# Linear attention and two MLPs on one core: a third chunk buffer, one load of the decays, weights loaded into their place, and an order of engines written out for the first layer

## The chip, the core and the metric

The kernel runs on one core of a Trainium2 chip. The metric is the time of one execution on the device in microseconds (us), as the median of several executions. One more execution is taken by the hardware profiler; its page and its trace are what is read below. The engines of the core are PE (matrix multiply, with its weight loads as PEld), DVE (VectorE), ACT (ScalarE), POOL (GpSimd) and SP (SyncE, which here issues the DMAs).

## What is computed

A gated linear attention over 4 x 8 heads of 768 tokens with head size 48, then two MLPs over 3072 tokens (width 384, inner width 2048), the first with the gate h * sigmoid(1.702 h), the second with h - tanh(h). All in float32.

```python
for t in range(S):
    state = alpha[:, :, t, :, None] * state + einsum('bhd,bhe->bhde', k[:, :, t], v[:, :, t])
    y[:, :, t] = einsum('bhd,bhde->bhe', q[:, :, t], state)
x = y.transpose(0, 2, 1, 3).reshape(B * S, H * D)
h = x @ w_in;   x = (h / (1 + exp(-1.702 * h))) @ w_out      # first MLP
h = x @ w_in2;  out = (h - tanh(h)) @ w_out2                 # second MLP
```

## The kernel before

**Attention in chunks.** A chunk is 128 tokens of one batch entry with all 8 heads, so there are 24 chunks (`NG`), six to a batch entry (`NCH`). Within a chunk the recurrence is written as matrix products: `a_scan` makes running products of the decays, one forward and one backward over the chunk (tensor_tensor_scan on DVE), `a_scale` multiplies k and q by them, PE makes the scores k by q (`a_scores` for chunks 0 to 7, two halves of eight matmuls each, `a_whole` for the later ones), a mask is laid on (a select on POOL, or a multiply on DVE at L301 in `a_whole`), and `a_out` makes the outputs: L325 with the carried state, L332 from scores and v, L341 the addition to the state, which `a_state` folds in on DVE. `a_guard` sums squares of the decay products on ACT for a check of range. For chunks from 8 on (`FULL`), `a_scale` runs on POOL and `a_turn` transposes k on DVE, 16 small transposes a chunk.

**Through memory and back.** `a_evac` copies a chunk's outputs from PSUM (ACT, L360) and stores them with four DMAs (L365) to a DRAM tensor; `a_back` reads them back token-transposed (L378); `a_x` splits x into a high part (ACT, L382) and a low part (DVE, L383) in the reduced float32 format that PE multiplies fast.

**The MLPs in blocks and steps.** Tokens go in six blocks of 512 for each layer, and a block has 16 steps, one for each 128 of the inner width; 192 steps in all. Step s makes nine matmuls of `gemm1` (L392: three parts of the contraction, each as high*high, high*low, low*high), then the activation (`sig_1`, L406, ACT) and its split (`g_split`: ghi on ACT at L409, glo on DVE at L410), and the nine matmuls of `gemm2` (L399) for step s - 3 (`LAG`).

**Weights.** They come as float64 bits. `w_load` fetches 768 KB into one of three `raw` buffers, `w_bits` and `w_join` make float32 on DVE (L163, L164, L176), `w_split` gives whi (ACT, L193) and wlo (DVE, L194). `conv` advances this pipeline by one weight at each call. `w_check` tests the exponents of a weight (DVE, then ACT) after loading it a second time.

**What runs when.** Chunks 0 to 3 are done ahead of block 0. During the steps of block j of the first layer the four chunks of block j + 1 are worked on (`attend`, `a_done`), so block 0 has chunks 4 to 7 and all the weight conversions between its steps, and blocks 1 to 4 have four chunks each. The checks of the first layer's weights lie in blocks 2 and 3, eight in each. The second layer's weights are converted in block 5 and in the second layer's first block.

**Buffers.** Two chunk buffers (`late`) and, for chunk 2 alone, a third place in tiles that are free at the start. `a_done(g)` loads chunk g + 2. The decays of a chunk are loaded twice, in reversed and in forward order (2 x 516 of 2056 columns).

**Order.** `in_order(begin)` fixes the order of each engine as the code emits it up to the end of block 0; behind that a scheduler orders the instructions by its own planning.

Of the kernel before, what the change touches and what calls it, by code (L numbers as in the profile page):

```python
# [17 lines left out]
C = 128  # L18
# [14 lines left out]
QW = 2 * AW + NP * C + NP * CE  # L33
# [35 lines left out]
def linear_attention_mlps(ctx, tc, xq, xv, fa, fv, cst, w1, w2, out):  # L69
# [10 lines left out]
    whi = [T(f"whi{m}", (128, WC), F32R) for m in range(MT)]  # L80
    wlo = [T(f"wlo{m}", (128, WC), F32R) for m in range(MT)]
    raw = [T(f"raw{i}", (128, WC, 2), I32) for i in range(3)]
# [18 lines left out]
    AR = 7184  # L101
# [15 lines left out]
    COLS = (AW, AW, NP * CE, NP * C, VW)  # L117
    lateb, late = [], []
    for _ in range(2):
        lateb.append(carve(QW))  # L120
        cuts = [0]
        for c in COLS[:4]:
            cuts.append(cuts[-1] + c)
        late.append([lateb[-1][:, u:v] for u, v in zip(cuts, cuts[1:])] + [carve(VW)])
    late0 = lateb[0]
    xsf = xs.rearrange("p k t -> p (k t)")
    third = [gt[:, 0:AW], gt[:, AW : 2 * AW], xsf[:, 0 : NP * CE], xsf[:, NP * CE :][:, :NB], gt[:, 2 * AW : 2 * AW + VW]]
# [27 lines left out]
    def w_load(layer, m):  # L155
        return SP.dma_start(out=raw[m % 3], in_=wsrc[layer][m].bitcast(I32).rearrange("p (n t) -> p n t", t=2))
# [4 lines left out]
    def w_bits(l, m):  # L161
        r, f = raw[m % 3], cfs[l][m % len(cfs[l])]
# [5 lines left out]
    def w_check(l, m):  # L168
        t = wt[m % 2]
        tc.keep_in_program_order(V.tensor_scalar(out=t, in0=w_high(raw[m % 3]), scalar1=0x3800, scalar2=0x7800,  # L170
# [3 lines left out]
    def w_join(l, m):  # L174
        r, f = raw[m % 3], cfs[l][m % len(cfs[l])]
        V.scalar_tensor_tensor(out=f.bitcast(I32), in0=r[:, :, 0], scalar=29, in1=f.bitcast(I32), op0=ALU.logical_shift_right, op1=ALU.bitwise_or)  # L176
# [13 lines left out]

    def w_split(l, m):
        f = cfs[l][m % len(cfs[l])]
        A.copy(whi[m], f)  # L193
        V.tensor_tensor(out=wlo[m], in0=f, in1=whi[m].bitcast(F32), op=ALU.subtract)  # L194
# [3 lines left out]

    def src(g, n):
        return (third if g == 2 else late[(g + (g > 2)) % 2])[n][: DP if n < 4 else 128]  # L200

    def dec(g, n):
        return src(g, n)
# [4 lines left out]
    def dec3(g, n):  # L208
        return pairs(dec(g, n))
# [16 lines left out]
    def a_load(g, parts=range(5)):  # L226
        if g == 0 and 0 in parts:
            for n in range(2):
                SP.dma_start(out=src(0, n), in_=xq[0, :, n * AW : (n + 1) * AW])
        elif 0 in parts:  # L230
            t = gt if g == 2 else lateb[(g + (g > 2)) % 2]
# [542 lines left out]
```

## Time and profile before

| | us |
|---|---|
| median of 3 runs | 953.19 (952.18 to 955.78) |
| profiled execution, its own time | 957.78 |
| its span | 956.1 |
| PE busy | 913.8 |
| DVE busy | 676.5 |
| ACT busy | 449.5 |
| POOL busy | 85.9 |

A line of the timeline tells when an instruction started (us from the start of the span), how long it took, its engine and line, what it writes and reads, how many of a kind are merged into the line, and in square brackets how long the engine had been idle before and who released it. Matmuls overlap in their pipeline, so the distance from one start to the next is what a matmul costs, and the time given is its latency. SPq lines are DMA issues. The windows give busy times of each engine in a stretch, with the number of instructions, and the granted clock of TensorE as a share of full speed (PEclk), which is also recorded as full where the trace has no clock record, as in the first 52 us.

### The profile page before, as it was taken

Reading aid. Unit: us, or ns where it says so; the run is one execution under the profiler, and the core shown is the slowest. Engines: PE = TensorE matmul, PEld = TensorE weight load, DVE = VectorE, ACT = ScalarE, POOL = GpSimd, SP = SyncE. Lnnn points to the kernel's source line nnn. Section 1 sums busy time; section 2 is a strip of 40 time slices with the busy share of each in tenths; the row PEclk is TensorE's granted clock in tenths of the full one; section 3 lists DMA queues with packets and bytes.
Section 4 is the critical chain, followed back from the end, with each engine's and each line's share of the span. In section 5 each row is a group of like instructions: output and inputs, shape, how many; then the busy total and the mean of one; then the engine's idle time right before and its main releaser. Section 6 shows DMA issues by size and latency. Waiting matters only on the chain.

```text
span 956.1 us, 13257 instructions
## 1 busy us (share of the span) xinstructions
PE 913.8 (96%) x4870; PEld 728.1 (76%) x4870; DVE 676.5 (71%) x1124; ACT 449.5 (47%) x906; POOL 85.9 (9%) x70
## 2 busy tenths in 40 slices
PE   5569999999989999999999999999999999999997
PEld 4347777777768777777888888888888888888885
DVE  7799997844774787484159986766776777766663
ACT  4445533323434434343344564554566566544542
POOL 1201211101120111110100200100100001000000
PEclk9999999989989999999999999999999999999999
DMA  9767434422643565434125410200322420000001
GB/s 268 236 201 240 137 87 125 120 68 79 200 132 141 159 196 198 128 113 158 32 93 181 138 60 1 78 22 1 113 96 89 166 99 1 33 1 1 34 1 37
DMA packets 58107, 101.91 MB, mean 107 GB/s; under 512 B 5024, under 2 KB 37408, under 8 KB 58032
## 3 DMA queue, kind: packets, MB, share of 16 engines
q1 hardware_dynamic: 58032, 100.97, 33.7%
q8 instruction: 40, 0.66, 0.3%
q14 instruction: 35, 0.29, 0.1%
HBM read 86.79 MB, written 14.16 MB: 106 GB/s over the span
## 4 chain that ended last, share of the span: by engine, by line
PE 61%; DVE 0%; issue 0%; ACT 0%; ACTq 0%
PE bank L399 30%; PE bank L392 29%; PE bank L332 1%; PE bank L298 0%; PE bank L325 0%; PE bank L341 0%; DVE xs L442 0%; DVE arena L301 0%; PE bank L268 0%; ACT xs L445 0%; ACTq L671 0%
## 5 line engine op out<-in xcount | busy, mean ns | idle before, releaser
L410 DVE TENSOR_TENSOR glo<-gt,ghi 128x512 fp32r<-128x512 f32 x192 | 140.1, 732 | 151.0 <-ACT ghi L409 146.8
L392 PE MATMUL bank<-xhi,whi 128*128 128x512 f32 x576 | 229.2, 398 | 9.5 <-ACT xhi L382 8.8
L399 PE MATMUL bank<-ghi,whi 128*128 128x512 f32 x576 | 233.1, 405 | 0.0
L399 PE MATMUL bank<-ghi,wlo 128*128 128x512 f32 x576 | 229.0, 397 | 0.0
L392 PE MATMUL bank<-xlo,whi 128*128 128x512 f32 x576 | 228.5, 397 | 0.4 <-DVE xlo L383 0.4
L399 PE MATMUL bank<-glo,whi 128*128 128x512 f32 x576 | 228.5, 397 | 0.0
L392 PE MATMUL bank<-xhi,wlo 128*128 128x512 f32 x576 | 228.1, 396 | 0.0
L409 ACT CAST ghi<-gt 128x512 fp32r<-128x512 f32 x192 | 119.2, 621 | 220.8 <-DVE gt L421 133.1
L392 PEld LDWEIGHTS bank<-xhi,whi 128*128 128x128 f32 x576 | 109.2, 190 | 35.6 <-ACT xhi L382 9.0
L399 PEld LDWEIGHTS bank<-ghi,whi 128*128 128x128 f32 x576 | 109.2, 190 | 28.4 <-issue 1.9
L392 PEld LDWEIGHTS bank<-xlo,whi 128*128 128x128 f32 x576 | 109.3, 190 | 26.4 <-DVE xlo L383 1.2
L399 PEld LDWEIGHTS bank<-glo,whi 128*128 128x128 f32 x576 | 109.4, 190 | 25.7
L392 PEld LDWEIGHTS bank<-xhi,wlo 128*128 128x128 f32 x576 | 109.1, 189 | 25.5
L399 PEld LDWEIGHTS bank<-ghi,wlo 128*128 128x128 f32 x576 | 109.5, 190 | 24.2 <-issue 0.5
L406 ACT ACTIVATE gt<-bank 128x512 f32<-128x512 f32 x96 | 57.4, 597 | 95.6 <-PE bank L392 72.0
L308 DVE STREAM_TRANSPOSE cf<-arena 32x128 f32<-32x128 f32 x256 | 77.5, 303 | 24.9 <-PE bank L341 10.0
L419 DVE SCALAR_TENSOR_TENSOR arena<-arena,bank 128x512 f32<-128x512 f32 x96 | 65.8, 686 | 29.4 <-ACT arena L417 28.6
L421 DVE SCALAR_TENSOR_TENSOR gt<-arena 128x512 f32<-128x512 f32 x96 | 68.3, 712 | 10.9 <-DVE arena L420 1.4
L417 ACT ACTIVATE arena<-bank 128x512 f32<-128x512 f32 x96 | 57.3, 597 | 36.1 <-PE bank L392 35.7
L243 DVE TENSOR_TENSOR_SCAN arena<-arena,seg 112x516 f32<-112x516 f32 x46 | 63.5, 1380 | 14.6 <-DMA arena<-xq 13.6
L418 ACT ACTIVATE arena<-arena,cs 128x512 f32<-128x512 f32 x96 | 69.6, 725 | 2.9
L420 DVE SCALAR_TENSOR_TENSOR arena<-arena 128x512 f32<-128x512 f32 x96 | 67.9, 707 | 3.0
(89 smaller groups left out, 663.2 us busy)
## 6 DMA issues: line engine op xcount, KB each, us to landing
raw<-w SPq DMA_DIRECT2D x64, 768.0 KB, 4.5
arena<-xq SPq DMA_DIRECT2D x46, 224.0 KB, 4.4
arena<-xq SPq DMA_DIRECT2D x22, 451.5 KB, 5.1
xlo<-xt SPq DMA_DIRECT2D x24, 192.0 KB, 4.4
x1t<-xs SPq DMA_DIRECT2D x6, 768.0 KB, 3.4
arena<-x1t SPq DMA_DIRECT2D x6, 768.0 KB, 4.5
out<-xs SPq DMA_DIRECT2D x18, 256.0 KB, 2.3
arena<-xv SPq DMA_DIRECT2D x23, 192.0 KB, 3.3
```

Of the source, the lines that this page charges most:

```text
L243: V.tensor_tensor_scan(out=dec(g, n), data0=src(g, n), data1=seg, initial=0.0, op0=ALU.mult, op1=ALU.max)
L308: V.transpose(out=d[32 * y : 32 * y + 32], in_=k[32 * x : 32 * x + 32, :, 32 * y : 32 * y + 32])
L392: P.matmul(out=h, lhsT=w[m][:, ws], rhs=x[:, k, :n], start=c == 0, stop=c == 3 * KT - 1)
L399: P.matmul(out=acc[k][:, :n], lhsT=w[m][:, ws], rhs=x[s % 3][:, :n], start=m == 0 and c == 0, stop=m == MT - 1 and c == 2)
L406: A.activation(out=gf[i][:, :n], in_=h, func=AF.Silu, scale=1.702)
L409: A.copy(ghi[s % 3][:, :n], gf[s % 2][:, :n])
L410: e.tensor_tensor(out=glo[s % 3][:, :n], in0=gf[s % 2][:, :n], in1=ghi[s % 3][:, :n].bitcast(F32), op=ALU.subtract)
L417: A.activation(out=u, in_=h, func=AF.Square, accum_out=usum[:, s - NS1 :][:, :1])
L418: A.activation(out=w, in_=u, func=AF.Square, bias=pbias)
L419: V.scalar_tensor_tensor(out=p, in0=u, scalar=P3, in1=h, op0=ALU.mult, op1=ALU.mult)
L420: V.scalar_tensor_tensor(out=p, in0=u, scalar=-PR, in1=p, op0=ALU.add, op1=ALU.mult)
L421: V.scalar_tensor_tensor(out=gf[i], in0=w, scalar=PD, in1=p, op0=ALU.add, op1=ALU.mult)
```

## The change

- The decays of a chunk are loaded once, in forward order, into 517 columns whose last is set to zero by a memset; the backward scan reads them with a negative step. `a_load` has four DMAs, for decays, q, k and v.
- Chunks from 3 on take three buffers in turn (`place_of`): the two of `late` and `spare`, which lies in the memory of two `raw` buffers. `a_done(g)` loads chunk g + 3.
- In the first layer a weight is loaded by `w_given` into the memory where its whi and wlo will lie, all 16 without a ring. The second load for the check goes to the third `raw` buffer.
- The checks of the first layer lie in blocks 1 to 4, four a block, each two steps behind its load.
- The start is written anew: all loads of chunks 0 to 3 first, the constants on ACT's DMA queue, the activation table loaded at the start, the scores of chunk g + 1 ahead of the outputs of chunk g, and `idle(n)`: n matmuls of 512 columns into an unused bank, 18 at the start, then 14, and 4, 3, 5 and 38 behind the outputs of chunks 0 to 3. Two of chunk 3's stores go to ACT's DMA queue. Three weights are converted by the start of block 0, with the bits of a fourth (before: three, a fourth joined and the bits of a fifth).
- In block 0, chunks 4 to 7 begin at steps 2, 5, 8 and 11 (before 0, 3, 6, 9), and `conv` stands at the end of a step.
- In blocks 1 to 4, `steady` places a chunk's parts at steps d = 0, 1, 2 and 5 from its begin (steps 0, 3, 7, 10 of the block). `in_order` now reaches to the end of block 4.

```diff
+    def place_of(g):
+        return third if g == 2 else (spare, *late)[g % 3] if g > 2 else late[g]
...
     def a_scan(g, n):
         if n == 0:
             V.memset(first, 1.0)
-        V.tensor_tensor_scan(out=dec(g, n), data0=src(g, n), data1=seg, ...)
-        if n == 0:
+            V.tensor_tensor_scan(out=dec(g, 0), data0=src(g, 1)[:, AW:0:-1], data1=seg, ...)
             V.reciprocal(out=first, in_=dec3(g, 0)[:, :, C:])
+        else:
+            V.tensor_tensor_scan(out=dec(g, 1), data0=dec(g, 1), data1=seg, ...)
...
     def a_done(g, b=5):
         a_evac(g, b)
-        if g + 2 < NG:
-            a_load(g + 2)
-        if g < FULL:
-            a_back(g)
+        a_back(g)
+        if g + 3 < NG:
+            a_load(g + 3)
...
+    STARTS = (0, 3, 7, 10)
+    def steady(g, d):
+        if d == 0:
+            if g == FULL:
+                a_turn(g, 0)
+            prep(g + 1, 0)
+            a_whole(g, 5)
+        if d == 1:
+            a_turn(g, 1)
+            prep(g + 1, 1)
+            prep(g + 1, 2)
+            prep(g, 3)
+        if d == 2:
+            if g + 1 < NG:
+                a_turn(g + 1, 0)
+            a_out(g, 5)
+            a_state(g)
+            a_done(g)
+        if d == 5:
+            x_hi(g)
+            x_lo(g)
...
+    def idle(n):
+        w = seg[:, 1:65].bitcast(BF16)
+        for _ in range(n):
+            P.matmul(out=bank[2], lhsT=w, rhs=w.unsqueeze(1).to_broadcast([DP, 4, 128]), start=True, stop=True)
...
     for r in range(3):
         prep(0, r)
+    idle(18)
+    for r in range(2):
+        s_mm(0, r, (5, 3)[r])
+    for x in range(4):
+        s_copy(0, x % 2, (5, 3)[x % 2], x > 1)
+    idle(14)
     for g in range(4):
         if g < 3:
             for r in range(3):
                 prep(g + 1, r)
+            for r in range(2):
+                s_mm(g + 1, r, (5, 3)[r])
...
         a_out(g, 0)
+        idle((4, 3, 5, 38)[g])
+        if g < 3:
+            for x in range(4):
+                s_copy(g + 1, x % 2, (5, 3)[x % 2], x > 1)
+        else:
+            w_hi(1, 0)
+        a_evac(g, 0, A if g == 3 else SP)
...
+            if l == 1 and 0 < j < len(L1) - 1 and m - 2 in STARTS:
+                w_check(1, 4 * (j - 1) + STARTS.index(m - 2))
+            if l == 1 and 0 < j < len(L1) - 1 and m in STARTS:
+                w_load(1, 4 * (j - 1) + STARTS.index(m), 2)
...
-        if s == MT - 1:
+        if s == (len(L1) - 1) * MT - 1:
             in_order(begin)
```

## Rows read from the trace of the kernel before

**Rows 1.** The page, part 1: busy time, share of the span, instructions of each engine.

```profile
PE 913.8 (96%) x4870; PEld 728.1 (76%) x4870; DVE 676.5 (71%) x1124; ACT 449.5 (47%) x906; POOL 85.9 (9%) x70
```

**Rows 2.** Timeline of the start: start us, us, engine, line, operation, [idle before <-releaser].

```profile
22.18 2.72 PE L279 MATMUL bank<-xs 48*128 48x176 f32 x16
30.31 2.72 PE L279 MATMUL bank<-arena 48*128 48x176 f32 x16
37.86 0.65 ACT L360 COPY wtb<-bank 112x256 f32<-112x256 f32 x2
38.26 2.61 SPq L365 DMA_DIRECT2D xt<-wtb  x4
47.41 0.80 PE L392 MATMUL bank<-xhi,whi 128*128 128x512 f32 x1 [8.79 <-ACT xhi L382]
```

**Rows 3.** Windows, blocks 0 to 5: length, busy by engine, PEclk, DMA share, GB/s.

```profile
47.41:136.35 88.94, 81.30 (x486) 62.22 (x486) 84.01 (x131) 45.27 (x99) 13.32 (x12) 0.96 0.60 178
136.35:222.98 86.63, 84.60 (x530) 66.56 (x528) 58.37 (x126) 29.59 (x55) 9.75 (x8) 0.96 0.31 89
222.98:310.21 87.23, 84.19 (x529) 66.59 (x528) 56.23 (x124) 35.29 (x70) 10.68 (x8) 0.96 0.49 151
310.21:392.64 82.43, 81.50 (x514) 64.04 (x513) 58.45 (x125) 35.06 (x70) 10.06 (x8) 1.00 0.56 174
392.64:473.42 80.78, 80.78 (x530) 64.18 (x528) 40.81 (x81) 29.78 (x56) 7.79 (x7) 1.00 0.33 106
473.42:540.34 66.92, 66.92 (x289) 54.26 (x288) 50.23 (x62) 30.91 (x49) 3.50 (x4) 1.00 0.39 130
```

**Rows 4.** Timeline of blocks 1 and 2, DVE and PE: two waits of PE.

```profile
185.56 1.23 DVE L243 TENSOR_TENSOR_SCAN arena<-arena,seg 112x516 f32<-112x516 f32 x1 [0.88 <-DMA arena<-xq]
188.45 2.27 DVE L243 TENSOR_TENSOR_SCAN arena<-arena,seg 112x516 f32<-112x516 f32 x1
191.35 0.42 PE L325 MATMUL bank<-arena,state 48*48 48x128 f32 x4 [1.45 <-DVE arena L301]
277.98 1.69 PE L325 MATMUL bank<-arena,state 48*48 48x128 f32 x16 [3.04 <-DVE arena L301]
```

**Rows 5.** Timeline of PE in block 0: dense and attention matmuls.

```profile
50.31 0.63 PE L392 MATMUL bank<-xhi,whi 128*128 128x512 f32 x1
50.73 0.63 PE L392 MATMUL bank<-xlo,whi 128*128 128x512 f32 x1
110.29 0.87 PE L279 MATMUL bank<-arena 48*128 48x176 f32 x8
115.46 0.66 PE L325 MATMUL bank<-arena,state 48*48 48x128 f32 x16
116.04 1.08 PE L332 MATMUL bank<-arena 128*48 128x128 f32 x16
116.95 0.53 PE L341 MATMUL bank<-arena 128*48 128x48 f32 x16
117.41 0.50 PE L399 MATMUL bank<-ghi,whi 128*128 128x512 f32 x1
```

**Rows 6.** Timeline of DVE in the start: chunk 0's first scan, chunk 1's memset.

```profile
4.19 1.23 DVE L243 TENSOR_TENSOR_SCAN arena<-arena,seg 112x516 f32<-112x516 f32 x1 [0.79 <-DMA arena<-xq]
8.05 0.06 DVE L242 MEMSET seg<- 112x4 f32 x1
```

**Rows 7.** Timeline of DVE in block 0: a weight's split, bits, and glo.

```profile
59.71 1.11 DVE L194 TENSOR_TENSOR wlo<-xs,whi 128x768 fp32r<-128x768 f32 x1
61.62 0.55 DVE L163 TENSOR_SCALAR cf<-raw 128x768 int32<-128x768 int32 x1
63.07 0.68 DVE L410 TENSOR_TENSOR glo<-gt,ghi 128x512 fp32r<-128x512 f32 x1
```

**Rows 8.** Timeline of POOL in the start: the select alone, and beside scans.

```profile
10.66 0.64 POOL L285 TENSOR_SCALAR_AFFINE_SELECT arena<-arena 128x512 f32<-128x512 f32 x1 [10.15 <-ACT arena L283]
24.58 2.81 POOL L285 TENSOR_SCALAR_AFFINE_SELECT arena<-arena 128x512 f32<-128x512 f32 x2 [5.33 <-ACT arena L283]
```

## What the change will do to the time

> **What bounds the kernel now.** I read the page first, then the timeline of the start for PE's longest wait, then PE's time block by block. By the page PE is the long engine, busy 913.8 of 956.1 us, and DVE comes next with 676.5 [rows 1]. So only two things can shorten the run: PE starting its main stream earlier, and PE not waiting inside it. The longest wait of PE is 8.79 us for the x of the first block, at 47.41 [rows 2]. The windows cut the span where the first L392 matmul of a block starts [rows 3]: the main stream starts at 47.41 and block 0 (16 steps of 18 matmuls, with the scores and outputs of chunks 4 to 7 between) takes 88.94 us. Blocks 1 to 4, with four chunks each, take 86.63, 87.23, 82.43 and 80.78. Block 5, without attention, takes 66.92, or 4.18 a step and 0.232 a matmul. In block 4 PE is busy 80.78 of 80.78 and the granted clock is 1.00, so that is what a block with four chunks costs when nothing waits. From 473.42 on nothing of the change touches PE, and I leave it as it is: 482.6 us to the end.
>
> Where blocks 1 and 2 lose time, the timeline shows one pattern [rows 4]. A scan at 185.56 waits 0.88 us for its load, the next scans (one of them 2.27 us long) and the mask multiplies queue behind it on DVE, and PE waits 1.45 us for the masks at 191.35. At 277.98 the same wait is 3.04 us. After each, the granted clock falls: 0.96 in those blocks against 1.00 in block 4. One such event costs the whole excess of its block, 86.63 - 80.78 = 5.85 and 87.23 - 80.78 = 6.45 us, so three quarters or half of the price is the clock and the rest the wait.
>
> **The change, part by part.** *Three buffers, loads three chunks ahead.* A chunk's load is now issued a whole chunk (about 20 us in blocks 1 to 4) before its scan, where it landed too late by 0.88 us. The DMA share in blocks 1 to 4 is 0.31 to 0.56 [rows 3], so there is room. The loads wait on SP for the buffer of a chunk that is already finished, so what stands behind them (the next chunk's stores, x read-back) is not held.
>
> *The fixed order in blocks 1 to 4.* I followed one chunk through the new order: masks are written in its first step and read in its third, the transposes in the second, the state update behind its own output matmuls, x two steps after its read-back is due. Every operand of PE is made at least one step (4.18 us) before its matmul. DVE is busy 40.81 to 58.45 us of a block [rows 3], so it has the time. The tightest place is the last chunk of a block: its x split ends about where the next block's first matmul starts; I allow nothing for it and put 1 us a block into the range. Gain: 5.85 + 6.45 + 1.65 (block 3) = 13.95 us.
>
> *Weight checks, four a block instead of eight in two blocks.* Each brings one reload on SP, one DVE and one ACT instruction; the reload stands two steps ahead of its check, on a buffer of its own. In block 4 DVE is idle for half the block. Cost nothing; if the reload were late, the DVE instruction would hold glo of its step, which PE needs two steps later.
>
> *The start.* Before, the attention of chunks 0 to 3 runs at PE's low clock: two dense matmuls at 50.31 and 50.73 are 0.42 us apart, against 0.232 later, which is the 1.2 GHz level against the 2.4 GHz one [rows 5]. The score matmuls of a chunk take 2.72 us and a chunk 8.13 (22.18 to 30.31) [rows 2]. At the high level the same matmuls cost 0.80 for half the scores, then 0.58, 0.91 and 0.46 by start to start [rows 5], so a chunk is 3.55 us of PE. The new kernel puts idle matmuls ahead and between and runs the scores of the next chunk before the outputs of this one. Then DVE sets the pace: one chunk's scans and scales take from 4.19 to 8.05, 3.86 us [rows 6], and with the state update and some contention I take 4.6, between 3.86 and 8.13. The four extra memsets (0.06 each, [rows 6]) hide in the 0.79 us that the first scan waits for its load. The reversed scan has no row. Its bounds are a scan alone, 1.23, and the longest scan, 2.27 [rows 4, 6]; I take 1.23, since the elements are as many. First outputs: 8.05 + 4.6 (chunk 1 scaled) + 1.6 (its scores) + 1.4 = 15.7; those of chunk 3 end 3 x 4.6 later, at 29.5. Before, from chunk 3's copies (37.86) to the first L392 matmul (47.41) is 9.55 us, of which 2.61 are four store issues on SP; two of them now go to ACT's queue, -1.3 [rows 2]. So x is there at 29.5 + 8.25 = 37.8. The 38 idle matmuls after chunk 3 have no row either; by the dense rows they take 38 x 0.232 = 8.8 us, or 16.0 at 0.42. I take 8.8: 29.5 + 8.8 = 38.3. **Block 0 starts at 38.2**, 9.2 us earlier.
>
> *Block 0.* Its step 3 needs weight 3 split. After x of chunk 3 (split by 38.2) DVE has in order: scans and scales of chunk 4 (3.86), the state update (two instructions on 192 columns, between nothing and two glo of 512 columns, 1.36: I take 0.7), then bits of weights 3 and 4 (1.45 each), one glo (0.68), and join and split of weight 3 (1.91) [rows 6, 7]: 10.0 us, so 48.2. PE's steps 0 to 2 take 3 x 2.09 + 0.80 = 7.1 and end at 45.3, so PE waits 2.9 us there. That is what comes next in place of the old 8.8. By [rows 4] a wait of 1.45 us was enough for a fall; I charge half of one, 1.7. The other 13 steps cost 13 x 4.18 + 4 x 1.95 (outputs) + 7 x 0.80 (scores) + 1.7 (what block 4 has over its rows) = 69.4. Block 0 ends at 48.2 + 69.4 + 1.7 = **119.3** instead of 136.35. DVE just keeps up: a weight costs 3.36, a glo 0.68, a third of a chunk 1.6, so 5.6 us a step against PE's 5.3, with the first and last steps lighter. Bounds: 114.4, if PE never waits, and 124, if DVE sets every step with another 0.3 us of contention.
>
> **The sum.** 136.35 - 119.3 = 17.05, and 13.95 in blocks 1 to 3: 31.0 us. The profiled execution took 957.78 us (1.7 around its span): 926.8. The median of the runs shown is 953.19, 4.6 lower than that execution. One clock event is 5.85 to 6.45 us, so I take the 4.6 to be such an event that comes in some executions; the changed kernel has none of them and keeps 926.8. If it is something else, the time is 4.6 lower, which the low end holds.
>
> **A rule weighed against a row.** In the start the mask select on POOL lies beside DVE's scans. Alone it takes 0.64 us; two beside a scan take 2.81 [rows 8]. *The Trainium skill, "SBUF — State Buffer", section "Who interferes with whom", says that a DVE instruction with two SBUF inputs and a GpSimd instruction that reads SBUF exclude each other for their whole length.* The rows agree with that in size: 2.81 is 1.4 each, which is 0.64 and most of a scan. In the new start every select meets a scan or a scale, since DVE is never free there. It is the third rival below.
>
> **Rivals.** *The clock stays low in the start* (chance 0.20, 936 us). For it: PE was at 1.2 GHz for the first 50 us though the window's matmuls followed each other closely, and between chunks only 3 to 5 idle matmuls stand. Then a chunk keeps its 8.13: outputs of chunk 3 end at 15.7 + 24.4 = 40.1, and the 38 idle matmuls take 8.8 to 16.0, so block 0 starts at 48.9 to 56.1, say 52. PE finds all weights ready and takes 7.1 + 69.4: 128.5, 9.2 later than my sum: 936. Against it: 18 dense matmuls stand ahead, and in the kernel before it was the first dense stream, from 47.41 on, that brought the high level.
>
> *The change does not do what it says in blocks 1 to 4* (0.10, 934 us): the scans no longer wait for loads, but the fixed order brings another wait in one or two chunks. Half of 13.95 stays: 933.8.
>
> *Scans and selects exclude each other* (0.08, 931 us): per chunk two selects of 1.4 and DVE longer by 2 x 0.64: 1.1 us on each of four chunks, and the start is 4.4 us later: 931.2.
>
> *Slower* (0.05, 970 us). The order is no longer planned but written out, so one misplaced DVE or ACT instruction would repeat in each of the 16 chunks of blocks 1 to 4: the masks behind a scan, say, with PE behind the masks, as in [rows 4]. Each event costs 5.85. Up to five are paid by the gain of 31.0, from the sixth on the kernel is slower; with seven or eight it is 31.0 - 7.5 x 5.85 = -12.9 against before, 970 us. Against it: the chunk that I followed has a step of slack everywhere, and 55 us of DVE work in 80.
>
> **How the numbers follow.** My forecast, 926.8, has 0.57; its own range is 918 to 932 (block 0's bounds, and 4.6 down). The range 918 to 939 adds the second and third rival and most of the first; outside lie the slow case (0.05), the late end of the first (0.06) and what may be lower (0.05). About 0.5% (5 us) can be told from no change. Faster by more: 0.95. Within: 0.01. Slower: 0.04, from the last rival.
>
> **What would show it.** The first L392 matmul at 37 to 40 us, with score matmuls at 0.80 for eight in chunks 1 to 3, shows the start right; 1.6 for eight shows the first rival. A wait of PE of some 3 us before step 3, for wlo, shows the DVE bound of block 0; none, with block 0 near 76.5 us, would put me 3 to 5 us too high. Blocks 1 to 4 at 80.8 each, at a granted clock of 1.00, show the buffers and the order right; one at 86 with a PE wait for a DVE line refutes it there. From block 5 on all windows should be the same as before.

## The result, and the profile after

The changed kernel takes 929.46 us (median of 4 runs, 929.32 to 930.21), the kernel before beside it 954.18 (4 runs, 952.18 to 955.78): a ratio of 0.974, interval 0.972 to 0.977. The forecast was 926.8, range 918 to 939. The profiled execution took 929.32 us with a span of 927.6; that of before was 957.78 with 956.1, so the two traces differ by 28.5 us, while the medians differ by 24.7: the profiled execution of before was 3.6 us slower than its median.

Lines of the changed kernel: a gemm's first matmul is L419 (before L392), its second L426 (L399), the scores L294 (L279) and, from chunk 8 on, L323 (L298), the outputs L350, L357 and L366 (L325, L332 and L341), the transposes L333, x split L402 and L406 (L382 for its high part), a weight's high part L204 and its low part L208 (L194), the scans L258 and L261 (L243), the masks L326 (L301), the stores L388 (L365), the read-back L398 (L378), the sigmoid of a step L433, a weight check L179 and L181, an idle matmul L575. L270 is ACT's activation of `a_guard` over a prepared chunk.

First the page of the kernel after: busy time of each engine (compare [rows 1]).

```profile
PE 910.0 (98%) x4952; PEld 716.3 (77%) x4952; DVE 669.0 (72%) x1128; ACT 447.9 (48%) x908; POOL 90.6 (10%) x70
```

PE is busy 98% of a shorter span. Next the timeline of its start (start us, us, engine, line, operation, idle before and releaser), the scores of chunks 0 and 3 (compare [rows 2]).

```profile
8.46 1.47 PE L294 MATMUL bank<-arena 48*128 48x176 f32 x16 [1.03 <-ACT raw L243]
...
22.72 1.47 PE L294 MATMUL bank<-raw 48*128 48x176 f32 x16 [0.76 <-ACT wtb L383]
```

A chunk's scores take 1.47 us where [rows 2] have 2.72. The same view from the last outputs to step 3 of block 0:

```profile
29.74 8.45 PE L575 MATMUL bank<-seg 112*128 112x512 bf16 x38
...
30.70 2.29 ACTq L388 DMA_DIRECT2D xt<-wtb  x2
...
33.03 0.51 ACT L402 CAST xhi<-xlo 128x384 fp32r<-128x384 f32 x1 [2.37 <-DMA xt<-wtb]
...
38.23 0.83 ACT L204 CAST w<-cf 128x768 fp32r<-128x768 f32 x1 [3.54 <-DVE cf L185]
...
38.97 0.92 ACT L402 CAST xhi<-xlo 128x384 fp32r<-128x384 f32 x2
...
39.94 0.49 PE L419 MATMUL bank<-xhi,w 128*128 128x512 f32 x1 [1.75 <-ACT xhi L402]
...
45.65 1.06 ACT L270 ACTIVATE arena<-arena 112x1032 f32<-112x1032 f32 x1 [4.70 <-DVE arena L266]
...
46.71 0.58 ACT L433 ACTIVATE gt<-bank 128x512 f32<-128x512 f32 x1
...
47.34 0.50 PE L419 MATMUL bank<-xhi,w 128*128 128x512 f32 x1 [2.08 <-ACT gt L433]
...
50.05 0.95 DVE L208 TENSOR_TENSOR w<-xs,w 128x768 fp32r<-128x768 f32 x1
```

Block 0 begins at 39.94. Three waits are to be seen. ACT stands 2.37 us at its own DMA queue ahead of the x split at 33.03. Then x of chunks 2 and 3 (38.97) stands behind weight 2 (38.23), and PE waits 1.75 us for it. At 47.34 PE waits 2.08 us for the first sigmoid (46.71), which stands on ACT behind the L270 of chunk 4 (45.65). The low part of weight 3 ends at 51.0, just after step 3 began at 50.42.

Last the windows of the kernel after, blocks 0 to 6 (length, busy by engine, granted clock, DMA share, GB/s; compare [rows 3]).

```profile
39.94:122.40 82.46, 77.63 (x486) 58.90 (x486) 77.73 (x109) 43.58 (x98) 13.71 (x10) 1.00 0.64 204
122.40:202.84 80.44, 80.44 (x530) 63.80 (x528) 54.45 (x127) 31.75 (x62) 10.81 (x8) 1.00 0.38 114
202.84:283.09 80.25, 80.25 (x530) 63.88 (x529) 52.46 (x120) 31.73 (x62) 10.82 (x8) 1.00 0.37 114
283.09:362.92 79.83, 79.83 (x514) 63.43 (x512) 51.94 (x118) 31.74 (x62) 10.94 (x8) 1.00 0.38 115
362.92:446.85 83.93, 83.93 (x545) 66.64 (x543) 58.80 (x122) 34.35 (x66) 12.31 (x9) 1.00 0.44 144
446.85:510.55 63.70, 63.70 (x274) 51.24 (x273) 49.01 (x61) 30.32 (x48) 2.22 (x2) 1.00 0.39 135
510.55:577.75 67.20, 67.20 (x289) 54.05 (x288) 51.15 (x72) 37.26 (x73) 5.47 (x4) 1.00 0.13 47
```

The granted clock is 1.00 in all of them. Blocks 1 to 3 cost 80.44, 80.25 and 79.83 us with PE busy throughout, where [rows 3] have 86.63, 87.23 and 82.43. Blocks 4 and 5 cut a little differently (83.93 + 63.70 = 147.63, before 80.78 + 66.92 = 147.70). From block 6 on a block takes 67.20. The gain of 28.5 us lies so: block 0 ends at 122.40 instead of 136.35 (13.95, of which 7.47 is its earlier start), blocks 1 to 5 take 388.15 instead of 403.99 (15.84), and what follows takes 1.3 more.

### The profile page after: what moved, and what is told of

Read it like the earlier page. It is cut to its first block, busy times and chain, and to the rows that moved or that the text cites. A ratio compares the mean times of both kernels' runs of the same rounds, so it can differ in the third digit from the quotient of the medians.

```text
span 927.6 us, 13395 instructions
## 1 busy us (share of the span) xinstructions
PE 910.0 (98%) x4952; PEld 716.3 (77%) x4952; DVE 669.0 (72%) x1128; ACT 447.9 (48%) x908; POOL 90.6 (10%) x70
## 3 DMA queue, kind: packets, MB, share of 16 engines
HBM read 81.28 MB, written 14.16 MB: 103 GB/s over the span
## 4 chain that ended last, share of the span: by engine, by line
PE 94%; DVE 2%; DMA 2%; ACT 1%; issue 1%; ACTq 0%; SPq 0%; DVEq 0%
PE bank L426 44%; PE bank L419 42%; PE bank L357 2%; PE bank L323 2%; PE bank L350 1%; PE bank L294 1%; PE bank L366 1%; DMA arena<-xq 1%; DMA xt<-arena 1%; DMA cs<-cst 0%; PE bank L575 0%; DVE arena L258 0%; DVE w L208 0%; DVE xs L173 0%; DVE xs L185 0%
## 5 line engine op out<-in xcount | busy, mean ns | idle before, releaser
L419 PE MATMUL bank<-xhi,w 128*128 128x512 f32 x1152 | 392.3, 395 | 4.3 <-ACT gt L433 2.1
L426 PE MATMUL bank<-ghi,w 128*128 128x512 f32 x1152 | 366.9, 399 | 0.0
L419 PEld LDWEIGHTS bank<-xhi,w 128*128 128x128 f32 x1152 | 216.2, 188 | 57.1 <-ACT gt L433 2.5
L426 PEld LDWEIGHTS bank<-ghi,w 128*128 128x128 f32 x1152 | 212.9, 188 | 53.0 <-issue 2.1
L419 PE MATMUL bank<-xlo,w 128*128 128x512 f32 x576 | 227.9, 396 | 0.6 <-DVE seg L257 0.6
L426 PE MATMUL bank<-glo,w 128*128 128x512 f32 x576 | 227.7, 396 | 0.0
L419 PEld LDWEIGHTS bank<-xlo,w 128*128 128x128 f32 x576 | 108.3, 188 | 27.2 <-DVE seg L257 0.9
L426 PEld LDWEIGHTS bank<-glo,w 128*128 128x128 f32 x576 | 108.2, 188 | 26.5
L433 ACT ACTIVATE gt<-bank 128x512 f32<-128x512 f32 x96 | 57.7, 601 | 108.5 <-PE bank L419 105.9
L485 POOL TENSOR_TENSOR xlo<-arena,xhi 128x512 fp32r<-128x512 f32 x18 | 28.0, 1584 | 339.6 <-ACT xhi L484 339.6
L333 DVE STREAM_TRANSPOSE cf<-arena 32x128 f32<-32x128 f32 x176 | 53.2, 302 | 2.5
L181 ACT ACTIVATE wtb<-wtb 128x768 bf16<-128x768 int16 x32 | 26.8, 839 | 43.5 <-DVE wtb L179 43.5
L406 DVE TENSOR_TENSOR xlo<-xlo,xhi 128x384 fp32r<-128x384 f32 x24 | 14.0, 586 | 33.0 <-ACT xhi L402 33.0
L333 DVE STREAM_TRANSPOSE cf<-raw 32x128 f32<-32x128 f32 x80 | 24.2, 302 | 1.1
```

The source lines that it names most:

```text
L333: V.transpose(out=d[32 * y : 32 * y + 32], in_=k[32 * x : 32 * x + 32, :, 32 * y : 32 * y + 32])
L419: P.matmul(out=h, lhsT=w[m][:, ws], rhs=x[:, k, :n], start=c == 0, stop=c == 3 * KT - 1)
L426: P.matmul(out=acc[k][:, :n], lhsT=w[m][:, ws], rhs=x[s % 3][:, :n], start=m == 0 and c == 0, stop=m == MT - 1 and c == 2)
L433: A.activation(out=gf[i][:, :n], in_=h, func=AF.Silu, scale=1.702)
L485: G.tensor_tensor(out=xlo[i][:, k], in0=xr[:, k], in1=xhi[i][:, k].bitcast(F32), op=ALU.subtract)
```

## The experiments

The table cuts every profiled execution the same way. "Places" says whether the parts of a chunk's attention in blocks 1 to 4 stand where the change puts them (new) or in 11 steps as before (old); "fixed to" is the last block whose order is written out, and beyond it the planner decides; "ahead" is how many chunks ahead a load is issued.

| kernel | places | fixed to | ahead | block 0 begins | ends | blocks 1 to 5 | span | ratio to before (95%) |
|---|---|---|---|---|---|---|---|---|
| before | old | 0 | 2 (two buffers) | 47.41 | 136.35 | 403.99 | 956.1 | 1 |
| after | new | 4 | 3 | 39.94 | 122.40 | 388.15 | 927.6 | 0.9744 (0.9722–0.9765) |
| e3_load_two | new | 4 | 2 | 39.87 | 122.46 | 388.15 | 928.0 | 0.9749 (0.9728–0.9771) |
| e4_order0 | new | 0 | 3 | 41.38 | 129.94 | 393.30 | 940.2 | 0.9865 (0.9843–0.9888) |
| e9_load_two_order0 | new | 0 | 2 | 41.21 | 124.71 | 395.37 | 937.3 | 0.9831 (0.9804–0.9858) |
| f2_packed_two | old | 0 | 2 | 41.06 | 130.84 | 407.66 | 955.7 | 1.0041 (1.0020–1.0062) |
| f1_packed_three | old | 0 | 3 | 40.96 | 129.41 | 407.49 | 954.3 | 1.0038 (1.0023–1.0052) |
| f3_packed_fixed | old | 4 | 3 | 39.62 | 122.05 | 514.97 | 1052.7 | 1.1059 (1.1013–1.1106) |
| e6_checks_bunched | new | 4 | 3 | 39.55 | 122.15 | 401.42 | 940.8 | 0.9906 (0.9880–0.9933) |

### Are the early loads the cure? e3_load_two

My theory was that a chunk's load, issued a chunk earlier, removes the pattern of [rows 4].

```diff
-        if g + 3 < NG:
-            a_load(g + 3)
+        if 7 <= g + 2 < NG:
+            a_load(g + 2)
```

> One edit: a chunk is loaded two chunks ahead instead of three (as in the kernel before), the rest as changed, the fixed order too. Theory (the early load is what takes the waits out of blocks 1 to 4): the load of chunk g + 2 is issued some 5 to 6 us behind the outputs of chunk g and lands 4.5 us later, while the scan of g + 2 is due about 3 us behind them where chunks stand three steps apart; so the scan waits up to 7 us, masks and transposes of the next chunk queue behind it on DVE, and PE waits some 2 us for them at two of the four chunks of a block: 8 waits, with the clock's share 15 to 30 us, 945 to 960 us; blocks 1 to 4 at 84 to 88 us. Rival (the fixed order alone is enough, with two steps between masks and outputs to take the late scan in): DVE waits for DMA but PE does not, blocks at 80.2 to 81, 930 us.

Measured: 929.91 us (929.71 to 930.1). Blocks 1 to 5 are 80.44, 80.25, 79.83, 83.93 and 63.70, equal to the kernel after to a hundredth. Yet the loads were late. DVE's waits in blocks 1 to 4 of this kernel (us in total, times, longest):

```profile
DVE arena L258 <- DMA arena<-xq: 12.9, 5, 5.0
DVE raw L258 <- DMA raw<-xq: 5.7, 2, 4.6
```

So DVE stood 18.6 us for loads, up to 5.0 at a time, and PE none of it. The theory falls. Why PE doesn't wait is seen at the longest of these waits, in block 4 (timeline of e3, PE and DVE):

```profile
381.16 1.16 PE L323 MATMUL bank<-raw 48*128 48x128 f32 x16
...
386.28 1.23 DVE L258 TENSOR_TENSOR_SCAN arena<-arena,seg 112x516 f32<-112x516 f32 x1 [4.98 <-DMA arena<-xq]
387.64 1.26 DVE L326 TENSOR_TENSOR arena<-bank,cs 128x512 f32<-128x512 f32 x2
...
390.82 0.65 PE L350 MATMUL bank<-raw,state 48*48 48x128 f32 x16
```

The mask (L326) stands right behind the late scan on DVE, here as in the kernel after (`steady` at d = 0). But in the new places the outputs (L350) follow the scores (L323) by 9.7 us, and the mask is whole at 388.9, 1.9 us before PE wants it. Late loads cost nothing as long as they fit into this slack.

### Is it the fixed order? e4_order0 and e9_load_two_order0

In e4 the order is written out to the end of block 0 only; e9 is e4 with the loads of e3.

```diff
-        if s == (len(L1) - 1) * MT - 1:
+        if s == MT - 1:
             in_order(begin)
```

> One edit: the written-out order ends with block 0 (as in the kernel before), blocks 1 to 4 are ordered by the scheduler's planning; three buffers and loads three ahead stay. Theory (the early load is the cure): scans find their data, nothing queues behind a DMA wait, blocks 1 to 4 stay at 80 to 81 us, 929 to 931 us. Rival (the order is the cure): the planner still puts other DVE work in front of masks, PE waits of 1 to 3 us with a fall of the clock come back in one to three blocks, each 5.5 to 6.5 us: 935 to 945 us.

> Both edits together: loads two ahead and the written-out order only up to block 0, which is what blocks 1 to 4 had before. Both theories: the events of before come back there, 86 to 87 us in two blocks and 81 to 83 in the others, 938 to 944 us; the start keeps its gain (block 1 begins at 122 us).

Measured: 941.34 (940.45 to 941.96) and 938.64 (935.89 to 939.35). Blocks 2 and 3 keep 80.2 and 79.8 in both, so the fixed order isn't what holds them there. What is lost lies around the boundary of blocks 0 and 1. The timeline of e4 there, DVE, ACT and PE:

```profile
129.39 0.50 ACT L402 CAST xhi<-xlo 128x384 fp32r<-128x384 f32 x1
...
129.94 0.50 PE L419 MATMUL bank<-xhi,w 128*128 128x512 f32 x1 [2.21 <-ACT xhi L402]
...
130.17 2.63 DVE L333 STREAM_TRANSPOSE cf<-arena 32x128 f32<-32x128 f32 x8
...
132.83 1.23 DVE L258 TENSOR_TENSOR_SCAN arena<-arena,seg 112x516 f32<-112x516 f32 x1
...
136.61 0.56 DVE L406 TENSOR_TENSOR xlo<-xlo,xhi 128x384 fp32r<-128x384 f32 x1
...
137.23 0.50 PE L419 MATMUL bank<-xlo,w 128*128 128x512 f32 x1 [2.45 <-DVE xlo L406]
```

The planner puts transposes (L333) and a scan (L258) ahead of the x split: its high part was written at 129.39, its low part comes at 136.61, 7 us later, and PE waits 2.45 us at 137.23. The x split of a block's last chunk is what the prediction called the tightest place. A window of the same kernel behind the wait of 2.21 us at 129.94 (columns as above):

```profile
131.00:134.40 3.40, 3.40 (x10) 2.55 (x8) 3.18 (x8) 0.00 (x0) 0.20 (x1) 0.50 0.15 32
```

The wait is followed by 3.4 us at a granted clock of 0.50, the 1.2 GHz level, which costs another 1.7; from 137.9 the same comes again behind the wait of 2.45. Of e4's later end of block 0 (7.5 us) 1.4 is the start (ACT's DMA queue, below). The rest is the block itself, 88.56 us for 82.46: the planner has put 21 transposes, a chunk's scans and the scores of chunk 8 into it, all work of block 1, and DVE, which sets its pace, is busy 86.87 us for 77.73. PE waits 2.35 us there for a weight's low part (at 122.63), before the 2.21. Block 0 of the kernel before, 88.94 us, has 29 such transposes; that of the kernel after has none. So nearly all that block 0 became shorter hangs on the fixed order too. In e9 the same loss is shared out otherwise: block 0 takes 83.50, block 1 87.66, with one PE wait of 5.26 us for the low part of x. Loads two ahead are again no worse.

### Is it the places of the parts? f1, f2 and f3

The three kernels put the parts of a chunk in blocks 1 to 4 back into the old places: f1 under the planner with loads three ahead, f2 the same with two, f3 with the order fixed to the end of block 4.

```diff
+    def packed(g, r):        # r = 0..3: prep(g+1, 0), a_whole(g) | ... | a_out, a_state | a_evac, a_back, x_hi, x_lo
...
-                    for c in range(4):
-                        steady(t1 // C + c, m - STARTS[c])
+                    for r in range(min(16, -(-m * 16 // 11)), min(16, -(-(m + 1) * 16 // 11))):
+                        packed(t1 // C + r // 4, r % 4)
```

> Blocks 1 to 4 put back as they were before in three things: the chunk's parts packed into the first eleven steps of a block (masks and outputs some 1.4 steps apart, the x split right behind the read-back), the order left to the planner, loads two ahead. Start and block 0 stay as changed. All theories: the events of before come back, a PE wait behind a mask multiply or an x split with a fall of the clock, 86 to 88 us in two or three of blocks 1 to 4; 938 to 946 us.

> The same with one difference: loads three ahead. Theory of the prediction (the early load removes the events): scans no longer wait for DMA and blocks 1 to 4 go to 80 to 82 us, 5 to 14 us better than the run with loads two ahead. Rival, after the runs so far (where the parts stand and in which order counts, the load does not): the events stay, within 3 us of that run, at other places perhaps.

Measured: f2 957.47 (7 runs, 955.86 to 960.35), f1 956.0 (8 runs, 955.16 to 957.08). Against before no gain is left, and f2 was expected at 938 to 946: it missed by more than 11 us. Block 0 still ends 5.5 to 6.9 us before that of the kernel before; blocks 1 to 5 take 3.5 to 3.7 more than in its first trace (e0, a second execution of before, has 400.93 there for 403.99, so this difference is little more than its scatter). Nor do the events lie where before had them: blocks 1 to 4 take 96.10, 81.64, 81.82 and 80.90 in f2, 95.71, 81.74, 81.94 and 80.90 in f1, so nearly all is lost in block 1. Loads three ahead change 0.2 us in blocks 1 to 5; the medians differ by 1.5, with ranges that overlap. The timeline of f1 in block 1, DVE and PE:

```profile
182.13 1.16 PE L323 MATMUL bank<-arena 48*128 48x128 f32 x16
...
187.69 1.23 DVE L258 TENSOR_TENSOR_SCAN arena<-arena,seg 112x516 f32<-112x516 f32 x1 [0.55 <-DMA arena<-xq]
...
189.63 2.00 DVE L261 TENSOR_TENSOR_SCAN arena<-arena,seg 112x516 f32<-112x516 f32 x1
...
191.80 1.23 DVE L258 TENSOR_TENSOR_SCAN raw<-raw,seg 112x516 f32<-112x516 f32 x1
...
193.28 1.23 DVE L261 TENSOR_TENSOR_SCAN raw<-raw,seg 112x516 f32<-112x516 f32 x1
194.43 1.26 DVE L326 TENSOR_TENSOR arena<-bank,cs 128x512 f32<-128x512 f32 x2
...
195.15 1.70 PE L350 MATMUL bank<-arena,state 48*48 48x128 f32 x16 [6.06 <-DVE arena L326]
```

It is [rows 4] again, with a load wait of 0.55 only: the planner put four scans of two chunks ahead of the masks (L326), which come 12.3 us behind their scores (182.13). In the old places the outputs were due 7.0 us behind them (in other chunks of f1 5.8 to 8.3), and PE waits 6.06 us. At the boundary of blocks 0 and 1 it waits another 4.44 for the low part of x, as in e4. From f1 to e4, both under the planner and three ahead, the places alone are worth 407.49 - 393.30 = 14.2 us in blocks 1 to 5, 10.1 of it in block 1.

> Parts packed into eleven steps as before, loads three ahead, but the order fixed as written up to the end of block 4. Theory (the planner's order, with scans of two chunks ahead of a mask, makes the events; the places alone cost little): blocks 1 to 4 between 80 and 82 us, block 1 begins at 122.4, 929 to 933 us. Rival (masks and outputs need two steps between them whoever orders them): a PE wait for masks or transposes in each chunk, blocks at 84 to 90 us, 945 to 960 us.

Measured: 1054.41 us. The window of its block 1, then its timeline there, ACT and DVE:

```profile
122.05:234.16 112.11, 91.47 (x530) 71.44 (x528) 56.85 (x127) 32.26 (x64) 10.16 (x8) 0.88 0.27 82
```

```profile
144.36 0.52 ACT L402 CAST xhi<-xlo 128x384 fp32r<-128x384 f32 x1 [5.69 <-DMA xlo<-xt]
...
144.91 0.56 DVE L406 TENSOR_TENSOR xlo<-xlo,xhi 128x384 fp32r<-128x384 f32 x1 [9.34 <-ACT xhi L402]
```

In the old places the read-back's split stands right behind the stores. ACT waits 5.69 us for the read-back (issued at 141.64) with evacuations and sigmoids behind it, and DVE waits 9.34 for ACT. PE is busy 91 of 112 us at a clock of 0.88. A wait of ACT in that block, and two of PE in the whole run (us in total, times, longest):

```profile
ACT wtb L181 <- DVE wtb L179: 27.3, 4, 8.9
```

```profile
PE bank L426 <- ACT xs L472: 41.2, 4, 10.9
PE bank L350 <- DVE arena L326: 34.7, 8, 6.9
```

L181 is ACT's half of a weight check: DVE, late itself, makes ACT late there too, with the evacuation of the block before (L472) behind it. So a written-out order with parts in bad places costs 514.97 - 388.15 = 127 us over five blocks: the mechanism of the "slower" rival, on ACT as much as at the masks. Part of it is the old places meeting the change's own places for the checks, which f3 doesn't separate.

### Are the weight checks free? e6_checks_bunched

The change makes four checks a block, each two steps after its load. Here eight stand in block 2 and eight in block 3, each one step after its load, on the same single buffer.

```diff
-            if l == 1 and 0 < j < len(L1) - 1 and m - 2 in STARTS:
-                w_check(1, 4 * (j - 1) + STARTS.index(m - 2))
-            if l == 1 and 0 < j < len(L1) - 1 and m in STARTS:
-                w_load(1, 4 * (j - 1) + STARTS.index(m), 2)
+            if l == 1 and 2 <= j < 4 and m % 2:
+                w_check(1, 8 * (j - 2) + m // 2)
+            if l == 1 and 2 <= j < 4 and not m % 2:
+                w_load(1, 8 * (j - 2) + m // 2, 2)
```

> The first layer's weight checks go back to blocks 2 and 3, eight in each, a load in even steps and its check one step later, with one buffer. Theory (the place of the checks costs nothing either way, DVE has a third of these blocks free): blocks 1 to 4 as with the changed kernel within 0.5 us, 929.5 us. Rival (the check waits for its load and holds DVE, so masks or glo come late): blocks 2 and 3 longer by 1 us or more each, 932 to 940 us.

Measured: 943.69 us (6 runs, 942.53 to 948.54). DVE's wait for a reload, blocks 1 to 4 of this kernel:

```profile
DVE wtb L179 <- DMA raw<-w: 30.1, 6, 8.4
```

Six waits, up to 8.4 us; in the same stretch of the kernel after DVE waits for no reload. Blocks 2 to 4 take 84.73, 88.13 and 84.41 against 80.25, 79.83 and 83.93: 13.3 us. The checks are free as the change places them, not in themselves. e6 puts more of them into a block and shortens their lead at once, so which of the two costs the 13.3 us isn't shown.

### The start: e2_no_idle, e7_x_first, c4_start

e2 leaves out all idle matmuls, which are no part of what is computed. e7 splits x of chunks 2 and 3 ahead of weight 2. c4 does that too, issues all stores of chunk 3 on SP, and moves the L270 of chunk 4 from the start into step 2.

```diff
 e2 -        for _ in range(n):
 e2 +        for _ in range(0):
 e7      (w_hi(1, 2), w_lo(1, 2) moved from around x_hi(2) to behind x_lo(3))
 c4 -        a_evac(g, 0, A if g == 3 else SP)
 c4 +        a_evac(g, 0)
 c4      (as e7, and prep(4, 3) moved from the start into step 2)
```

> One edit: all idle matmuls left out (they only keep PE busy; nothing reads them). Theory (they hold PE at 2.4 GHz through the start): scores of a chunk take 2.7 us instead of 1.4 and the outputs twice their time, the attention of chunk 3 ends at 34 to 38 us instead of 29.7, the first block starts at 43 to 47 instead of 39.9 and its first step takes 4 to 5 us instead of 2.3; part of that is taken back, since PE then finds the weights ready: block 1 begins at 127 to 131 us instead of 122.4, 934 to 938 us. Rival (PE is not what paces the start, DVE is): first block at 40 to 41, block 1 at 123 to 125, 930 to 932 us.

Measured: 932.67 us (932.13 to 932.75), ratio 0.9776 (0.9754 to 0.9797). Block 0 begins at 43.19 and ends at 125.65, both 3.25 later; its length is 82.46 as after. Windows of e2 (columns as above):

```profile
19.20:32.80 13.60, 9.01 (x175) 7.06 (x172) 10.92 (x16) 9.78 (x30) 3.50 (x4) 1.00 0.78 222
32.80:43.19 10.39, 0.00 (x1) 0.01 (x1) 5.22 (x7) 3.37 (x7) 0.00 (x0) 0.50 0.70 224
43.19:49.90 6.71, 6.40 (x14) 4.73 (x15) 6.53 (x13) 2.01 (x4) 0.00 (x0) 0.50 1.06 321
```

Without any idle matmul the scores of chunks 0 and 1 take 2.72 us each, those of chunk 2, from 18.47, 1.85, and those of chunk 3, from 23.34, 1.47. So PE has the high clock from about 19.20 on (the granted clock is no help here, it reads 1.00 before 19.20 too, as where the trace has no clock record); it falls in the 10 us in which PE has nothing to do. The first matmuls of block 0 then run at 0.50 for 6.7 us, which block 0's length doesn't show, since DVE sets its pace there.

Of the 3.25 us only a part is PE's. Timeline of e2, ACT's DMA issue (compare 30.70 in the kernel after):

```profile
31.77 4.47 ACTq L388 DMA_DIRECT2D xt<-wtb  x2
```

The issue begins 1.07 us later and holds ACT 2.18 us longer (4.47 for 2.29). In all ten kernels here that keep these stores on ACT and x behind weight 2, block 0 begins 6.95 us (within 0.01) behind the end of this issue. So 1.07 us come from the slower PE and 2.18 from the queue, whose hold went from 2.02 to 4.08 in runs that keep the idle matmuls; whether leaving them out made it longer isn't shown.

> One edit ahead of block 0: the x splits of chunks 2 and 3 stand before the split of weight 2 in the order of ACT and DVE instead of behind or between. Theory (block 0 begins when x of chunk 3 is split, and that waits behind weight 2 on ACT): the first L419 matmul goes from 39.9 to 38.2 to 38.6, where the idle matmuls end, DVE gets to chunk 4 some 1.5 to 2 us earlier, and block 1 begins at 120.5 to 121 instead of 122.4: 927.5 to 928 us. Rival (block 0 is bound by all the work of DVE ahead of weight 3): block 1 at 122, 929 us.

Measured: 929.46 us (928.74 to 929.84), ratio 0.9755 (0.9733 to 0.9777). Block 0 begins at 38.88, 1.06 earlier, and ends at 122.24, 0.16 earlier. Timeline of e7:

```profile
44.50 0.68 DVE L266 TENSOR_TENSOR arena<-arena 112x512 f32<-112x512 f32 x1
...
45.22 1.06 ACT L270 ACTIVATE arena<-arena 112x1032 f32<-112x1032 f32 x1 [4.59 <-DVE arena L266]
...
46.91 0.50 PE L419 MATMUL bank<-xhi,w 128*128 128x512 f32 x1 [3.05 <-ACT gt L433]
```

DVE's chunk 4 (L266) ends at 45.18, as in the kernel after (45.62) within half a us; ACT's L270 waits for it, the sigmoid stands behind, and PE now waits 3.05 instead of 2.08. What PE gained it waits out. Nor is the earlier beginning beyond doubt: l1, whose start is written as in the kernel after, began block 0 at 39.04.

> Three edits ahead of block 0: all stores of chunk 3 on SP's queue, x of chunks 2 and 3 split ahead of weight 2, the guard of chunk 4 behind the first activations instead of ahead of them. Theory (ACT stood 2.3 us at its DMA queue, and DVE waited 3.2 us for x of chunk 0 because of it; DVE's work ahead of weight 3 sets block 0): DVE's wait shrinks to about 1 us, weight 3 is split at 48.5 instead of 51, block 1 begins at 119.5 to 120.5 instead of 122.4: 927 us. Rival (the stores on SP delay x of chunk 3, which sets it): first L419 matmul later than 39.9 and block 1 at 122 to 123, 929 to 930 us.

Measured: 928.44 us (928.07 to 928.8), ratio 0.9737 (0.9705 to 0.9768). Block 0 begins at 38.09, 1.85 earlier, and ends at 121.65, 0.75 earlier. The wait for the sigmoid is gone; the timeline shows what is late next:

```profile
47.76 0.50 PE L419 MATMUL bank<-xhi,w 128*128 128x512 f32 x1 [1.96 <-ACT w L204]
...
49.83 0.73 PE L419 MATMUL bank<-xhi,w 128*128 128x512 f32 x2 [1.34 <-DVE w L208]
```

PE waits 1.96 and 1.34 us for the two halves of weight 3, as the prediction had it at 48.2, and from 50.7 on the granted clock is 0.50 for 6.8 us. It is the fastest kernel by about 1 us, but the interval of its ratio overlaps that of the change, and block 0 of the change itself (and of e3, e6 and l1, which start alike) ended between 121.5 and 122.5: whether c4 is better stays open.

### Why blocks 6 to 10 take 67.20: l1_alt and e0_before

In the first trace of before these blocks took 66.92 [rows 3]. l1_alt swaps the two halves of every second weight in its buffer, to see whether the place decides; e0 is the kernel before in another execution.

```diff
-            whi[m], wlo[m] = t[:, :WC], t[:, WC:]
+            whi[m], wlo[m] = (t[:, :WC], t[:, WC:])[:: 1 - 2 * (m % 2)]
```

> One edit: for odd weights the low half lies in front of the high half. It tests why a step of blocks 6 to 10 takes 67.20 / 16 us with the changed kernel and 66.92 / 16 before, although the instructions are the same. Theory (where the weights lie in SBUF sets a nanosecond of each matmul): the steps of these blocks change, to 66.9 a block if it is the parity of the weights' place, and the time falls by 3 us to 926.5. Rival (it is the chip or the execution): 67.20 stays, 929.5 us.

> The kernel before once more, profiled beside the others. Theory (the changed kernel's matmuls are some 0.9 ns slower, by something that it changed): blocks 6 to 10 take 66.92 us each here too, against 67.20. Rival (execution or chip): 67.20 here. And blocks 1 to 3 show which events of the first profile come back in another execution: if the 4.6 us between that profile and the median are one event, one of the three excesses is missing or smaller.

Measured: l1 929.46 us (928.39 to 930.15), blocks 6 on 67.20. e0 956.46 us; its windows, blocks 1 to 3 and 5:

```profile
136.24:218.63 82.39, 81.62 (x529) 64.18 (x528) 57.21 (x126) 29.48 (x55) 10.29 (x8) 1.00 0.32 94
218.63:304.41 85.78, 83.07 (x529) 65.76 (x528) 56.10 (x124) 35.47 (x70) 10.67 (x8) 0.98 0.49 154
304.41:389.12 84.71, 83.06 (x513) 65.39 (x512) 58.33 (x125) 35.25 (x70) 10.78 (x8) 0.98 0.56 173
...
469.97:537.17 67.20, 67.20 (x289) 54.05 (x288) 50.26 (x62) 30.91 (x49) 3.50 (x4) 1.00 0.37 129
```

The kernel before has 67.20 here, and f3, whose weights lie as in the kernel after, has 66.93. f3 and e0 ran on the same chip. So the pace belongs to the execution, not to the kernel. The same rows show that blocks 1 to 3 of before change places from one execution to another: 82.39, 85.78 and 84.71 here, 86.63, 87.23 and 82.43 in [rows 3].

## Why the prediction was right, and where not

**The sum.** The span was forecast at 925.1 and is 927.6. Block 0 ends at 122.40 instead of 119.3 (+3.1), blocks 1 to 5 take 388.15 instead of 390.04 (-1.9), the rest 417.05 instead of 415.76 (+1.3). Two slips in the working are small: block 0's lower bound is 45.3 + 69.4 = 114.7 and not 114.4, and the third rival takes 2 x 0.64 = 1.28 as 1.1 without a reason. The errors of blocks 0 and 1 to 5 partly cancel.

**What bounds the kernel**: right. Both gains lie where it looked, and PE is busy throughout blocks 1 to 6.

**The start**: right in mechanism. Scores at the high level, outputs of chunk 3 at 29.74 for 29.5. The first rival (clock low, 936 us) didn't come. Its price of 9.2 us wasn't tested: in e2, without idle matmuls, the clock was low only until 19.2 and again from 32.8, and of the 3.2 us lost 1.07 came from the slower PE. So most of the 7.47 us by which block 0 begins earlier doesn't hang on the idle matmuls but on how the start is ordered; which part of that order isn't shown.

**Two stores on ACT's queue, -1.3**: the gain didn't come. The queue held ACT for 2.29 us with x behind it, and in other executions of the same start for up to 4.08 (e4). Together with x behind weight 2 it put block 0 at 39.94 for 38.2. With all stores on SP (c4) block 0 began 0.79 us earlier than in e7, but c4 moves the L270 too, so that the stores on ACT lose time is likely and not shown. At block 0's end e7 and c4 were 0.2 and 0.8 us earlier than the change, no more than kernels that start alike differ, because DVE's work comes next.

**Block 0, a PE wait of 2.9 before step 3**: the size right, the path in part. DVE's work for chunk 4 does hold PE, but by way of ACT: PE waited 0.61 us for the low part of x at 41.04 and 2.08 for the first sigmoid, behind chunk 4's L270, which I hadn't followed; weight 3 came just in time (its low part at 51.0, the matmul that reads it at 51.05). In c4, where the sigmoid waits for nothing, the forecast wait for weight 3 comes in full (1.96 + 1.34). Step 3 began at 50.42 for 48.2, and this isn't DVE's list: from x split (41.0) to weight 3 whole (51.0) it took 10.0 us, as in the sum. It began 2.8 us late, since x was split at 41.0 and not by 38.2. The other 13 steps took 72.0 us with PE busy 69.84; I had 69.4, and 1.7 for a fall of the clock that didn't come, in place of which PE stood 2.1 us in short gaps. The sum doesn't say why block 0 gets shorter than its 88.94; by e4 the fixed order, which keeps transposes and scans of block 1 out of it, is most of the reason.

**Blocks 1 to 3, 13.95 from three buffers and the fixed order**: the size right (15.77), the cause half wrong. I read the 0.88 us load wait in [rows 4] as the root. By e3 loads can be 5.0 us late at no cost, and by f1 the pattern returns with loads three ahead. What matters is how much stands on DVE, a wait for a load included, between the scores and what PE needs from DVE, against the time until PE needs it: 9.7 us from scores to outputs in the new places, 5.8 to 8.3 in the old; and for x at the end of a block, which I allowed nothing for, the order alone decides (e4, e9). The new places give 14.2 us (f1 to e4), the fixed order another 5.2 in blocks 1 to 5 and most of 7.5 at block 0's end (e4 to after); with loads two ahead it is worth 9.3 of span (e9 to e3) against these 12.6. The fixed order without the places loses 98 us (f1 to f3). Loads three ahead against two are worth 0.4 of span, within the scatter. The third buffer itself stays in every run, and decays loaded once and weights landing in place weren't tried by themselves either; the page has 81.28 MB read for 86.79 before.

**The rival "fixed order brings another wait"** (934): not seen, nor the slower one (970), though f3 shows that its mechanism is real and that I priced it low.

**Scans and selects exclude each other** (931): the mechanism is there, the price is not. Two selects beside a scan took 2.55 us (from 10.05), 1.74 (from 20.34) in chunk 2, and the scales beside them 1.06 to 1.12 instead of 0.67; the scans kept 1.23. So the two hold each other up, yet the scores of chunks 0 and 3 begin at 8.46 and 22.72: a chunk takes 4.75 us, 0.15 over my 4.6 and not 1.1. The Trainium skill, "SBUF — State Buffer", section "Who interferes with whom", has the two exclude each other; the rows of the selects and scales agree with it, and only my sum of what it costs a chunk was too high, as the 4.6 already held some contention.

**Weight checks at nothing**: right as built. Of the two reasons given, DVE's idle time is not enough: e6 has the same work and loses 13.3 us. That leaves the lead of two steps, or that only four stand in a block.

**4.6 us between the profiled execution and the median**: I took it for a clock event that comes in some executions. That fits: 38 other runs of the kernel before lie from 950.1 to 957.6, and events move between blocks (e0), while the change's four runs lie within 0.9 us. It isn't proved that one event makes the 4.6.

**The tail unchanged**: right in kind; +1.3 is the pace of the execution (66.92 or 67.20 a block).

## What to carry to other kernels

Where a wait chain reads "load, scan, mask, PE", ask which link can be moved before making the first one earlier: here the load could be 5 us late for nothing, with the mask still behind the scan on DVE, once PE wanted the mask only 9.7 us after the scores. Writing out an order multiplies what the places are worth, in both directions: 12.6 us of span gained on good places, 98 lost on bad ones. When one cause of a wait in a start is removed, list what the next engine has queued behind it; undoing one of three delays here (e7) or all of them (c4) moved block 0 by 1 to 2 us at its beginning and 0.2 to 0.8 at its end.

## What the runs showed of the hardware

- A wait of PE is not followed by the same clock each time. After waits of 1.75 and 2.08 us in the kernel after, the granted clock stayed at 1.00, and the matmuls 0.23 us apart; after 1.45 us [rows 4] it was 0.58 over the next 8.1 us, after 2.21 us in e4 0.50 for 3.4 us, and after 3.05 us in e7 0.51 for 3.5 us. What decides stays open, and with it the price of one wait.
- A block without attention takes 66.92 or 67.20 us, from block 6 to block 10 of an execution the same. The kernel before had both, in two executions; the kernel after and its variants had 67.20, but for f3 with 66.93.
- Two stores on ACT's DMA queue held ACT for 2.02 us in l1, 2.29 in the kernel after and 4.08 in e4, with the same order of the start in all three. What sets the length stays open.
